# One block's 1226 tasks put in another written order (adaLN, linear attention and gated MLP on one core)

## The chip, the core and the metric

The kernel runs on one core of a Trainium2 chip. The core has TensorE (PE, matrix products, whose weight loads are shown apart as PEld), VectorE (DVE), ScalarE (ACT), GpSimd (POOL) and SyncE (SP, which here only issues DMAs). Each engine works through its own queue in order; semaphores make it wait for others. The metric is the device time of one execution in microseconds, as the median of several runs; lower is better.

## The reference

One transformer block on x of 2048 tokens by 512 (bf16), one batch, conditioned on a row c.

```python
mod = (_silu(c) @ w_mod).reshape(c.shape[0], 6, 1, -1)
sa, ca, ga, sb, cb, gb = (mod[:, 0].copy(), mod[:, 1].copy(), mod[:, 2].copy(), mod[:, 3].copy(), mod[:, 4].copy(), mod[:, 5].copy())
h = _layernorm(x, axis=-1) * (1 + ca) + sa
x = x + ga * _A_ref(h, A_wqkv, A_w_phi, A_wo)
h = _layernorm(x, axis=-1) * (1 + cb) + sb
x = x + gb * _B_ref(h, B_w_gate, B_w_up, B_w_down)
```

A is linear attention with 32 heads of 16: q, k and v by wqkv; pq and pk are q and k times a 16x16 matrix for each head; phi is softmax(p) beside softmax(-p) (32 features a head); kv sums phi_k by v over all tokens, z sums phi_k; the output of a head is (phi_q kv) / (phi_q z), then wo. B is a gated MLP of width 1376: (sigmoid(h w_gate) * (h w_up)) w_down.

## The kernel before

All work is cut into 1226 named tasks. `Graph.add` records for each task its engines (`alts`), what it reads and writes, and its buffers; `Graph.arrange` reads the long string `ORDER` (L40 to L87), gives each task its engine (the first of its alternatives, or the letter behind `@`: A for ACT, D for DVE, P for POOL), and hands out buffer slots in that order: 8 PSUM banks, 6 tiles `r2k`, 2 output tiles `ot`, and so on. `emit` then writes the instructions in that order. So ORDER alone sets each engine's queue, SP's DMA queue among them, and which earlier task must be done before a slot is used again.

The tasks, with the lines that the profile names:

- SP loads `ld_*`: `x0a` to `x3a` are tokens (256 KB for two tiles of 128, x3a 512 KB), `wk0`, `wk1` halves of the key weights, `wm00a` to `wm01b` the four 256 KB pieces of w_mod for sa and ca, `wmm2` 1.5 MB of w_mod for the rest, `wmga` the piece for ga, `wv0`, `wo`, `wu0`, `wg0`, `wd`, `wd2` weights. `wqT0` to `wqT3` (L798) are DMA transposes of the query weights from DRAM. `gwa`, `gra`, `gwb`, `grb` send ga and gb through DRAM to spread them over the partitions.
- `warm0` (six matmuls) and `warm1_0` to `warm1_11` (one each, L729) do no part of the result; PE runs them while it waits for data. `c1`, `c2`, `c3` make silu(c). `modc1.0` and `modc1.1` (L759) multiply it with w_mod for sa and ca and need wm00a with wm00b, and wm01a with wm01b; `modc2.0`, `modc2.1` (L745) need wmm2; `modca` needs wmga. Those with a c behind copy the result to SBUF.
- Key and query weights are folded with w_phi: `tpw` (L790) transposes, `wTc` (L793) copies, `fold` (L808) multiplies, `foldc` (L814) copies to `wqk_f`; side 1 is the keys, side 0 the queries.
- First layernorm over 16 token tiles, in nine groups (tiles 0; 1; 2,3; and so on): `st1` (L831, L832), `rs1` (L838 on ACT, L841 and L842 on POOL), `nmr1` (L847), `xn1` (L856, L860), transposes `tph` on PE (L873; for the groups of tiles 10 to 13 a DMA `xT1`, L865), `hm1` (L880 on ACT, L882 elsewhere) with the modulation.
- For each token tile t: `K` (L899; with a and b in two halves for t under 8), `e` (exp, ACT, L920), `n` (sums, DVE, L923), `r` (reciprocal; L936 on DVE, L933 and L934 on ACT), `phi` (product, POOL or DVE, L926), `V` (L903), `va` (copy, L949), `kv` (L287; adds into two PSUM banks over all tiles). Tiles 11, 13, 14 and 15 go in parts. Then `kvm`, `kvp`, `kvz`, `kvn` (L308 to L338) mask and reorder kv.
- `Q` and `qe` (L987, L992) for four chunks of 512 tokens by four blocks. Then for each unit of one or two tiles: `sm`, `smS`, `den` (L421 to L430) or, from tile 8 on, `z` and `dn` (L380 to L404); `num` (L457, L373), `u` (L463, L446, L448), `o` and `oT` (L481, a DMA transpose L484; on PE as `tpo` for tiles 0 and 1), `out` (L490), `x1` (L495, adds x), `st2` (L499, L500), `rs2`, `nmr2`, `xn2` (L532, L534), `xnT` (L541; on PE for tiles 0 and 1, L549), `mod` (L556 to L560). `wo` and `wd` (L967, L976) scale weights with ga and gb on POOL.
- MLP over six chunks of 1, 1, 2, 4, 4 and 4 tiles and eleven blocks of the width: `g` and `u` with a dot (L581, and L583, L586 for the last block), `tg` (tanh, ACT, L591), `hm` with a dot (DVE, L599 to L602), then `y` (eleven matmuls a tile, L619), `fin` (adds x, DVE, L626) and `st` (store, L628). The last tile, 15, goes in two parts, 384 columns and 128 columns (`b`).
- `bnd*` (L640 to L659) work out a bound on the weights and `ldf` reads the flag; above it another program part, `general`, would be run. It isn't run here.

What ORDER says goes through these two lines:

```python
t.eng = LETTER[e] if e else next(iter(t.alts))
assert t.eng in t.alts and t.deps <= done and t not in done, name
```

Of the kernel before, what the change touches and what calls it, by code (L numbers as in the profile page):

```python
# [1175 lines left out]
```

## Time and profile before

| | |
|---|---|
| median of 3 runs | 208.11 us (208.02 to 208.42) |
| span of the profiled execution | 207.1 us, mean granted TensorE clock 0.997 |
| PE, DVE, ACT, POOL busy, share of the span | 97%, 81%, 52%, 49% |
| DMA | 18.75 MB, mean 91 GB/s |
| instructions | 4382 |

In the fences below, a line of the timeline is: start in us, length in us, engine, line, operation, output and input by the program's names, shapes, count (neighbours of one kind are merged), and in brackets how long the engine sat idle just before and what ended that. A line of groups is: line, engine, operation, names, shapes and count, then busy us and mean ns of one, then idle us before them. A line of waits is: who waited, for whom, total us, times, longest. A line of stretches is: from and to, length, then busy us and count for PE, PEld, DVE, ACT and POOL, the granted clock, the share of the DMA engines and GB/s. A DMA issue line ends with the KB of one and the median us from issue to landing.

### The profile page before, as it was taken

Reading aid. Unit: us, or ns where it says so; the run is one execution under the profiler, and the core shown is the slowest. Engines: PE = TensorE matmul, PEld = TensorE weight load, DVE = VectorE, ACT = ScalarE, POOL = GpSimd, SP = SyncE. Lnnn points to the kernel's source line nnn. Section 1 sums busy time; section 2 is a strip of 40 time slices with the busy share of each in tenths; the row PEclk is TensorE's granted clock in tenths of the full one; section 3 lists DMA queues with packets and bytes.
Section 4 is the critical chain, followed back from the end, with each engine's and each line's share of the span. In section 5 each row is a group of like instructions: output and inputs, shape, how many; then the busy total and the mean of one; then the engine's idle time right before and its main releaser. Section 6 shows DMA issues by size and latency. Waiting matters only on the chain.

```text
span 207.1 us, 4382 instructions
## 1 busy us (share of the span) xinstructions
PE 200.2 (97%) x1559; PEld 112.0 (54%) x1559; DVE 167.1 (81%) x456; ACT 108.4 (52%) x266; POOL 100.7 (49%) x135
## 2 busy tenths in 40 slices
...
GB/s 169 319 354 300 266 195 75 143 257 327 54 0 3 51 6 51 54 51 29 76 103 17 89 0 25 36 68 52 38 38 0 52 79 25 51 25 3 25 63 51
DMA packets 32557, 18.75 MB, mean 91 GB/s; under 512 B 21169, under 2 KB 30738, under 8 KB 32530
## 3 DMA queue, kind: packets, MB, share of 16 engines
...
## 4 chain that ended last, share of the span: by engine, by line
PE 73%; DVE 9%; ACT 8%; DMA 3%; SPq 3%; issue 2%; POOL 0%; DVEq 0%; POOLq 0%
PE y_ps L619 18%; PE u_ps L581 17%; PE g_ps L581 17%; PE a_ps L490 7%; PE q_ps L987 5%; ACT e L920 4%; DMA x_sb<-in_A_x_dram 3%; DVE st L831 3%; DVE ks L923 3%; PE num L373 2%; PE num L457 2%; SPq L676 1%; ACT h1T L880 1%; PE g_ps L583 1%; ACT vaug L949 1%
## 5 line engine op out<-in xcount | busy, mean ns | idle before, releaser
L591 ACT ACTIVATE tg<-g_ps 128x512 bf16<-128x512 f32 (+3 forms) x66 | 28.4, 454 | 58.2 <-PE g_ps L581 40.7
L619 PE MATMUL y_ps<-wd_sb,wmod_sb 128*128 128x512 bf16 (+4 forms) x187 | 44.7, 367 | 0.0
L602 DVE SCALAR_TENSOR_TENSOR wmod_sb<-tg,u_ps 128x512 bf16<-128x512 bf16 (+4 forms) x63 | 30.1, 493 | 12.6 <-ACT tg L591 8.0
L581 PEld LDWEIGHTS <-wg_sb 128*128 128x128 bf16 (+1 forms) x252 | 21.7, 99 | 15.1
L581 PEld LDWEIGHTS <-wu_sb 128*128 128x128 bf16 (+1 forms) x252 | 21.6, 99 | 15.0 <-issue 0.4
L926 POOL TENSOR_TENSOR phi<-e,ks 128x1024 bf16<-128x1024 bf16 (+2 forms) x18 | 28.0, 1565 | 2.3 <-DVE phi L926 1.8
L619 PEld LDWEIGHTS <-wmod_sb 128*128 128x128 bf16 (+1 forms) x187 | 17.3, 98 | 16.4 <-issue 0.2
L481 POOL TENSOR_TENSOR o<-u 128x512 bf16<-128x512 f32 x12 | 15.2, 1270 | 22.4 <-DVE u L446 12.6
L581 PE MATMUL u_ps<-wT_sb,wu_sb 128*128 128x512 bf16 (+2 forms) x124 | 24.0, 322 | 0.0
L581 PE MATMUL g_ps<-wT_sb,wg_sb 128*128 128x512 bf16 (+2 forms) x124 | 23.6, 322 | 0.0
L581 PE MATMUL u_ps<-wqk_sb,wu_sb 128*128 128x256 bf16 (+4 forms) x128 | 19.9, 287 | 0.0
L923 DVE TENSOR_REDUCE ks<-e 128x64 f32<-128x1024 bf16 (+2 forms) x22 | 19.6, 896 | 0.2
L920 ACT ACTIVATE e<-k_ps 128x512 bf16<-128x512 f32 (+2 forms) x44 | 19.5, 547 | 0.3 <-PE k_ps L899 0.2
L581 PE MATMUL g_ps<-wqk_sb,wg_sb 128*128 128x128 bf16 (+4 forms) x128 | 19.1, 287 | 0.0
L626 DVE TENSOR_TENSOR ot<-y_ps,x 128x512 bf16<-128x512 f32 (+2 forms) x17 | 11.0, 654 | 8.8 <-PE y_ps L619 7.5
L992 ACT ACTIVATE eT<-q_ps 128x512 bf16<-128x512 f32 x32 | 17.2, 632 | 0.1
L899 PE MATMUL k_ps<-wqk_f,h1T 128*128 128x512 bf16 x64 | 16.8, 378 | 0.0
L903 PE MATMUL v_ps<-wv_sb,h1T 128*128 128x512 bf16 x64 | 16.3, 379 | 0.0
L490 PE MATMUL a_ps<-wo_sb,oT 128*128 128x512 bf16 x64 | 16.1, 379 | 0.0
L987 PE MATMUL q_ps<-h1T,wqk_f 128*128 128x512 bf16 x64 | 15.9, 379 | 0.1
L831 DVE BATCH_NORM_STATS2 st<-x_sb 128x6 f32<-128x512 bf16 x16 | 10.7, 668 | 3.1 <-DMA x_sb<-in_A_x_dram 3.1
L976 POOL TENSOR_TENSOR wd_sb<-wd_sb,wmod_sb 128x512 bf16<-128x512 bf16 x11 | 12.7, 1168 | 0.0
...
## 6 DMA issues: line engine op xcount, KB each, us to landing
out_dram<-ot SPq DMA_DIRECT2D x15, 128.0 KB, 1.7
...
wd_sb<-in_B_w_down_dram SPq DMA_DIRECT2D x1, 1280.0 KB, 10.4
...
```

What stands on the lines that cost most here:

```text
L490: pe.matmul(ap_[:], lhsT=oT[:, j, :], rhs=wo_sb[:, j, :], start=(j == 0), stop=(j == KT - 1))
L581: pe.matmul(ps[:fsz, 0:n], lhsT=w[:, j, ft * P:ft * P + fsz], rhs=h[:, j, 0:n], start=(j == 0), stop=(j == KT - 1))
L591: G.add(f"tg{k}.{ft}", {"ACT": 0.13 + n * 0.00083}, lambda e, tg=tg, g_ps=g_ps, fsz=fsz, n=n: act.activation(tg[:fsz, 0:n], g_ps[:fsz, 0:n ...
L602: dve.scalar_tensor_tensor(hm_all[:fsz, hm[k].slot, ft, 0:n], tg[:fsz, 0:n], 1.0, u_ps[:fsz, 0:n], op0=ALU.add, op1=ALU.mult)
L619: mm = pe.matmul(y[:, 0:c1 - c0], lhsT=hm_all[:fsz, hm[k].slot, ft, tl * P:(tl + 1) * P], rhs=wd_sb[:fsz, ft, c0:c1], start=(ft == 0), sto ...
L831: dve.bn_stats(st1[:, t, :], x_sb[:, t, :])
L899: pe.matmul(kp[:], lhsT=h1T[:, j, t * P:(t + 1) * P], rhs=wqk_f[:, j, D:2 * D], start=(j == 0), stop=(j == KT - 1))
L920: act.activation(ee[:, ha:hb, s, :], kp[:, ha * DH:hb * DH].rearrange("p (h j) -> p h j", j=DH), ACT.Exp, scale=1.0 - 2.0 * s)
L923: dve.tensor_reduce(ks[:, ha:hb].rearrange("p h s -> p (h s)"), ee[:, ha:hb].rearrange("p h s j -> p (h s) j"), axis=AX.X, op=ALU.add)
L926: engine(e).tensor_tensor(ph[:, ha * 32:hb * 32].rearrange("p (h j) -> p h j", j=DH), ee[:, ha:hb].rearrange("p h s j -> p (h s) j"), ks[: ...
L987: pe.matmul(qp[:], lhsT=wqk_f[:, j, blk * P:(blk + 1) * P], rhs=h1T[:, j, cq * 512:(cq + 1) * 512], start=(j == 0), stop=(j == KT - 1))
L992: act.activation(eT[cq][:, s * 4 + blk, :], qp[:], ACT.Exp, scale=1.0 - 2.0 * s)
```

## The change

ORDER is replaced as a whole; nothing else in the file is. The same 1226 tasks stand in another order, and 94 of them name another engine: 17 go from ACT to POOL, 14 from POOL to ACT, 26 from DVE to ACT, 26 from ACT to DVE, 7 from POOL to DVE and 4 from DVE to POOL. PE's tasks and the matmuls in them are the same. The beginning and the end of both strings:

```diff
--- before.py
+++ after.py
@@ -38,52 +38,52 @@
 ORDER = """
-wdz warm0 c1 warm1_0 warm1_1 warm1_2 warm1_3 warm1_4 ld_x0b st1_3 st1_2 c2 rs1_2 ld_x0a ld_wk1 tpw2 st1_1 rs1_1 pmem bd wTc2 tpw3 warm1_5 warm1_6 nmr1_2 st1_0
-c3 ld_wk0 wTc3 tpw0 tpw1 warm1_7 ld_x1a nmr1_1 st1_4 xn1_2 xn1_3 wTc0 rs1_0 ld_wm00a ld_wm00b xn1_1 ld_wm01a fold13 fold12 warm1_8 warm1_9 tph21 fold10 tph20
-st1_5 wTc1@D rs1_3@P ld_wm01b xn1_0 modc1.0 fold11 warm1_10 foldc13 foldc12 foldc10 modc1c0@D ld_x2a ld_x1b ld_wv0 hm1_20 hm1_21 warm1_11 tph01 tph03 tph00
-tph11 foldc11 hm1_00@A modc1.1 tph02 K3a modc1c1 hm1_01 nmr1_3 xn1_5 xn1_4 hm1_11@A st1_9 st1_8 rs1_5@P tph10 tph22 tph23 K2a K0a hm1_03@A hm1_02@A hm1_22@A
-K0b st1_7 st1_6 rs1_4@P tph30 tph33 ld_x2b hm1_23@A K3b V3a V3b K2b tph13 ld_x3a hm1_33 nmr1_5 e0.0 hm1_10@A st1_10 e3.0 tph12 V2a V2b V1a hm1_12@A va3
-hm1_13@A nmr1_4 n0.0 tph32 hm1_32 hm1_30 tph31 r0.0 xn1_9 n3.0 xn1_6 xn1_7 xn1_8 V0a V1b K1a tph42 V0b phi0.0 va2 hm1_31@A e2.0 va1 ld_wmm2 st1_11 va0 tph41
-K1b e1.0 tph40 r3.0@A K4a tph43 n2.0 K5a hm1_42 K5b tph53 hm1_53 modc2.0 rs1_6@P modc2.1 hm1_41@A hm1_43@A hm1_40@A modc2c r2.0@A n1.0 tph51 hm1_51 wqT0 wqT3
-ld_wmga tph52 kv0.0 K4b e4.0 V5 fold03 hm1_52@A nmr1_6 phi3.0 foldc03 e5.0 phi2.0 st1_15 r1.0 st1_13 st1_14 V4 va4 rs1_8 phi1.0 xn1_11 n4.0 nmr1_8 ld_wd wqT1
-ld_wd2 V6 modca.0 K6a modca.1 tph50 xn1_10@A modcac K7a K7b hm1_50 r4.0 kv1.0 kv2.0 K6b st1_12 K8 V9 e7.0 va6 e6.0 n5.0 xT1_10 xT1_11 rs1_7 va9 gwb wqT2 r5.0
-xn1_14 xn1_15 kv3.0 tph82 tph80 phi4.0 va5@D nmr1_7 hm1_80 K9 V7 e8.0 xn1_12@A xT1_12 kv4.0 V8 phi5.0 hm1_60 hm1_61 xn1_13@A xT1_13 n7.0 hm1_82 r7.0 n6.0
-kv5.0 hm1_62@P hm1_63@P K10 tph83 ld_wo e9.0 va7 V10 K11 tph81 hm1_83@A phi7.0 e10.0 va8@D r6.0 n8.0 hm1_81 phi6.0 r8.0 V11 fold02 V14 hm1_70 hm1_73 hm1_71
-foldc02 kv6.0 hm1_72@P phi8.0 K14 kv7.0 e11.0 n9.0 va14 e11.6 e11.2 e11.4 r9.0 K13 kv8.0 K12 n10.0 n11.0 r10.0 n11.6 n11.4 va10 e14.0 e14.4 wmod_free phi9.0
-n11.2 fold00 foldc00 r11.4 r11.2 r11.6 n14.0 V13 kv9.0 fold01 phi10.0 e12.0 foldc01 e13.0 va11 r11.0 va13@D r14.0 V12 gwa Q03 Q00 phi11.4 kv10.0 n12.0 phi11.2
-phi11.0 kv11.0 kv11.2 r12.0 qe03 e13.4 n14.4 r14.4@A ld_wu0 ld_wg0 grb va12 K15 kv11.4 phi11.6 e15.4 n13.0 r13.0 n13.4 V15 kv11.6 r13.4@A e15.0 qe00 Q10 Q01
...
-g5.7 tg5.7 hm5.1 g5.8 hm5.7 fin9 u5.8 g5.5 tg5.4 u5.0 y11.7 g5.10 st8 g5.0 y11.8 bnd0 bnd2 tg5.8 hm5.8 u5.5 tg5.0 hm5.0 y11.9 u5.4 hm5.4 bndb g5.3 tg5.5 tg5.3
-y11.10 fin11 hm5.5 u5.3 hm5.3 g5.6 u5.10 u5.6 tg5.6 hm5.6 y13.0 y13.1 y13.2 y13.3 y13.4 y13.5 y13.6 y13.7 tg5.10 y15.0b bndc hm5.10 st9 st11 bndd y15.1b y15.0
-y15.2b y15.1 y15.3b y15.4b y13.8 y13.9 y13.10 y15.5b y15.6b y15.7b fin13 y15.8b y15.2 y15.3 y15.4 y15.5 y15.6 y15.9b st13 y15.7 y15.8 y15.10b y15.9 y15.10
-fin15b y12.0 st15b fin15 st15 ldf y14.0 y14.1 y14.2 y14.3 y14.4 y14.5 y14.6 y14.7 y14.8 y12.1 y14.9 y14.10 fin14 st14 y12.2 y12.3 y12.4 y12.5 y12.6 y12.7
-y12.8 y12.9 y12.10 fin12 st12
+wdz warm0 c1 warm1_0 c2 warm1_1 ld_x0b pmem warm1_2 st1_3 st1_2 warm1_3 bd warm1_4 ld_x1a warm1_5 warm1_6 st1_5 st1_4 ld_wk0 tpw1 tpw0 rs1_2@P nmr1_2 rs1_3@P
+ld_x0a ld_wk1 wTc0 st1_1 wTc1 nmr1_3 xn1_3 fold10 xn1_5 tpw3 warm1_7 st1_0 rs1_0@P ld_x2a xn1_4 tpw2 foldc10 wTc3 fold13 warm1_8 c3 wTc2 fold12 ld_wm00a
+ld_wm00b st1_8 xn1_2@A rs1_1 nmr1_1 xn1_0 warm1_9 warm1_10 tph21 modc1.0 tph00 tph20 warm1_11 tph01 ld_wm01a ld_wm01b foldc12 st1_9 foldc13 xn1_1 modc1c0
+hm1_20@A fold11 tph03 tph30 foldc11 ld_x1b hm1_21 hm1_30 ld_x2b tph11 hm1_11 modc1.1 hm1_00@A tph10 tph12 tph32 tph22 modc1c1@D hm1_10 wqT0 ld_wv0 hm1_01@A
+rs1_5@P hm1_12@A hm1_03 nmr1_5 tph13 hm1_13@A xn1_9 xn1_8 K2a tph02 hm1_02@A hm1_22@A st1_6 st1_7 tph23 K3a hm1_23@A K0a tph33 K0b K1a hm1_32@A e0.0 K2b tph53
+tph52 K1b K3b rs1_4@P st1_10 st1_11 rs1_6@P hm1_53 hm1_33 nmr1_4 ld_x3a ld_wmm2 hm1_52@A e2.0 tph31 V0a e1.0 V1a V1b hm1_31 nmr1_6 tph51 n0.0 tph50 V0b fold00
+hm1_51 e3.0 foldc00 r0.0@A n1.0 hm1_50 xn1_7 V4 xn1_6 xn1_11 xn1_10 phi0.0 tph43 V2a tph40 wqT2 wqT1 n2.0 st1_14 hm1_43@A r1.0@A va4 va0 V3a V2b V3b hm1_40@A
+va2 tph41 K4a phi1.0 K5a r2.0 hm1_41 tph42 K4b n3.0 K5b hm1_42@A st1_15 e4.0 modc2.0 K6a va3 modc2.1 r3.0@A kv0.0 xT1_11 wqT3 phi2.0 xT1_10 ld_wmga ld_wu0
+rs1_8 va1 modc2c gwb phi3.0 e5.0 K9 K7a kv1.0 K7b fold02 n4.0 K8 kv2.0 V5 nmr1_8 r4.0 st1_13 phi4.0 st1_12 xn1_14 hm1_62 e7.0 n5.0 K6b V9 kv3.0 rs1_7 nmr1_7
+va5@D V8 e8.0 e9.0 xn1_13@A xn1_12 xT1_12 ld_wd2 r5.0 fold03 n7.0 kv4.0 xn1_15 va8@D foldc02 phi5.0 V7 e6.0 r7.0 foldc03@D hm1_60@P hm1_61 hm1_63 tph83 hm1_83
+V6 modca.0 modca.1 modcac va6 tph82 kv5.0 hm1_82@A n6.0 r6.0@A xT1_13 tph80 V11 K10 K11 hm1_71 n8.0 va7@D va9@D r8.0 phi7.0 tph81 hm1_81 n9.0 hm1_73 hm1_80@A
+hm1_70 hm1_72 e10.0 phi6.0 r9.0 V10 kv6.0 kv7.0 phi8.0 e11.2 e11.4 fold01 K15 foldc01 e11.6 va10 K12 e11.0 va11 kv8.0 e12.0 V13 phi9.0 n10.0 r10.0 phi10.0 K14
+n11.6 e14.4 n11.0 n11.2 r11.2 r11.0 phi11.0 kv9.0 V12 Q03 n11.4 r11.6 r11.4 n12.0 e15.4 e15.0 e14.0 va13 n15.0 r12.0 n15.4 phi11.6 phi11.2 phi11.4 phi12.0
+kv10.0 Q02 kv11.0 K13 kv11.2 V15 qe03 r15.0@A phi15.0 r15.4 n14.0 n14.4 r14.4 r14.0 Q12 kv11.4 kv11.6 e13.4 va12 n13.4 phi14.4@D phi15.4@D phi14.0@D e13.0
+qe02 r13.4@A va15 phi13.4 kv12.0 Q01 V14 va14 Q11 Q00 perm ld_wd Q10 kv13.4 kv14.4 qe01 n13.0 r13.0 phi13.0@D kv13.0 kv15.4 kv14.0 kv15.0 kvm1 Q31 gwa grb
+ld_wo wmod_free gra kvm0 wo3 wo1 kvp2 kvp1 kvn2 kvz1 qe00 qe10 qe11 kvp0 Q33 kvz0 kvz2 sm0 kvn0 qe31 sm2 smS0@D den0 Q13 kvn1@A num01 Q30 smS2 den2 num00 Q32
+num30 wd8 wo2 qe33 num31 u01 qe13 qe30 u00 u30 wd7 u31 wo0 wo_all num20 sm1 qe32 smS1 num21 num10 tpo0 Q20 num11 oT0 qe12 o3 den1 u21 u20 out0 Q21 sm4 u11
+qe20 qe21 smS4 oT3 ld_wg0 Q23 x1_0 wd10 o2 wd0 wd2 oT2 u10 tpo1 num71 num60 st2_0 den4 num70 num61 rs2_0 oT1 out3 nmr2_0 xn2_0 u70 u71 out1 xnT0 u61 mod00
+mod01 u60 tsw Q22 mod02@A mod03@A x1_1 out2 qe22 u0.8 g0.8 g0.6 tg0.8 g0.1 tg0.6 x1_3 u0.1 u0.7 u0.6 g0.4 hm0.8 x1_2 tg0.1 hm0.1 hm0.6 sm3 g0.0 g0.7 wd3 wd1
+u0.0 g0.9 o7 st2_1 oT7 qe23 g0.2 wd5 o6 tg0.0 tg0.7 hm0.0 hm0.7 rs2_1 st2_2 tg0.9 u0.9 hm0.9 nmr2_1 u0.3 g0.10 g0.3 oT6 tg0.3 tg0.2 xn2_1 out7 y0.0 u0.2 u0.4
...
+out15 tg4.6 rs2_7 hm4.4 nmr2_7 xn2_12 tg4.2 hm4.2 x1_15 st2_15 hm4.6 tg4.5 g4.7 u4.5 hm4.5 xn2_13@P g4.8 tg4.8 tg4.7 rs2_8 y11.1 g4.3 y9.0 y9.1 u4.8 u4.7
+xnT13 xnT12 st5 nmr2_8 mod73 hm4.8 xn2_14 xn2_15@P xnT14 xnT15 g4.9 u4.3 u4.10 tg4.3 hm4.3 y8.0 y8.1 g4.10 u4.9 tg4.9 hm4.7 tg4.10 hm4.10 mod71 hm4.9 st4
+y10.0 y10.1 y10.2 y9.2 y11.2 y11.3 y11.4 y10.3 y10.4 y11.5 y10.5 y10.6 y10.7 y10.8 y10.9 y10.10 fin10 st10 mod81@A y9.3 y8.2 y11.6 y11.7 y11.8 y11.9 mod82@P
+mod72 mod80 y8.3 y8.4 mod70@A mod83 g5.4 g5.9 tg5.9 tg5.4 g5.1 u5.4 u5.9 hm5.9 u5.3 hm5.4 y8.5 g5.0 g5.8 tg5.0 y8.6 y8.7 y8.8 y8.9 y8.10 u5.1 u5.0 tg5.1 hm5.1
+bnd1 g5.3 tg5.3 hm5.3 fin8 y11.10 g5.5 tg5.5 y9.4 u5.5 g5.6 u5.2 fin11 u5.8 bnd3 hm5.0 hm5.5 tg5.8 g5.2 u5.6 y15.0 g5.7 tg5.2 hm5.2 y13.0 y13.1 y13.2 y13.3
+bnd0 bndb tg5.6 st8 y9.5 y9.6 y9.7 y9.8 y9.9 y9.10 u5.7 hm5.8 st11 hm5.6 g5.10 tg5.7 u5.10 y13.4 bndc hm5.7 y13.5 y13.6 y12.0 y12.1 y13.7 y13.8 y13.9 y12.2
+tg5.10 y12.3 y12.4 y12.5 y12.6 bndd ldf hm5.10 y12.7 y12.8 fin9 st9 y14.0 y12.9 y12.10 y14.1 y15.1 y14.2 fin12 y13.10 st12 y14.3 y14.4 y14.5 y14.6 y15.2 y14.7
+y15.3 fin13 st13 y15.4 y14.8 y14.9 y15.5 y15.6 y14.10 fin14 y15.7 y15.8 y15.9 y15.10 fin15 st14 y15.0b y15.1b y15.2b st15 y15.3b y15.4b y15.5b y15.6b y15.7b
+y15.8b y15.9b y15.10b fin15b st15b
```

The loads, in SP's old order: x0b x0a wk1 wk0 x1a wm00a wm00b wm01a wm01b x2a x1b wv0 x2b x3a wmm2 wqT0 wqT3 wmga wd wqT1 wd2 xT1_10 xT1_11; in the new: x0b x1a wk0 x0a wk1 x2a wm00a wm00b wm01a wm01b x1b x2b wqT0 wv0 x3a wmm2 wqT2 wqT1 xT1_11 wqT3 xT1_10 wmga wu0. Seven Q tasks stand ahead of the first kv of tile 13 in the new order, five in the old. The last tile stored is 15b in the new order and 12 in the old.

44 lines of the change are left out of this document (17 added, 27 removed).

## Prediction

> **What bounds the kernel now.** I read the page's first two parts, then busy time by stretches, then the waits of TensorE (PE), then the timeline of the first 60 us.
>
> ```profile
> span 207.1 us, 4382 instructions
> PE 200.2 (97%) x1559; PEld 112.0 (54%) x1559; DVE 167.1 (81%) x456; ACT 108.4 (52%) x266; POOL 100.7 (49%) x135
> 5.00:10.00 5.00, 3.93 (x50) 2.52 (x48) 4.49 (x18) 4.29 (x12) 3.41 (x5) 1.00 1.12 319
> 13.10:58.00 44.90, 43.88 (x419) 24.42 (x418) 42.50 (x90) 43.03 (x112) 41.18 (x42) 1.00 0.82 206
> 58.00:203.80 145.80, 145.72 (x1042) 81.78 (x1040) 115.35 (x338) 57.46 (x136) 51.26 (x64) 1.00 0.18 40
> L619 PE MATMUL y_ps<-wd_sb,wmod_sb 128*128 128x512 bf16 x150 | 39.4, 379 | 0.0
> 203.76 0.69 DVE L626 TENSOR_TENSOR ot<-y_ps,x 128x512 bf16<-128x512 f32 x1 [1.26 <-PE y_ps L619]
> 204.48 0.33 SPq L628 DMA_DIRECT2D out_dram<-ot  x1
> out_dram<-ot SPq DMA_DIRECT2D x15, 128.0 KB, 1.7
> ```
>
> The window rows read: stretch, its length, then busy us of PE, PEld, DVE, ACT, POOL. From 58 us to the last matmul PE is busy 145.72 of 145.80 us: no order can win there, it can only lose. From 13.1 to 58 us every engine is over 90% busy, and PE loses 1 us that this view counts (a matmul's end is modelled, so it sees only part). So the time is PE's fixed work, what PE waits ahead of 58 us, and the tail: the last addition 203.76 to 204.45, a store issued at 204.48 that lands 1.7 us later (206.2), and 0.9 us to the end of the span. The profiled execution's span is 207.1 us and the median of the runs 208.11, so I make the sum against 207.1 and add 1.0 us.
>
> **The change part by part.** The set of tasks is the same and PE runs the same 1559 matmuls; 94 tasks outside PE change engine. What counts is where PE waits.
>
> *Landings.* The input loads land one after another in the order of issue.
>
> ```profile
> 6.11 0.62 PE L790 MATMUL tp_w<-ident,wqk_sb 128*128 128x128 bf16 x8 [0.63 <-DMA wqk_sb<-in_A_wqkv_dram]
> 7.22 0.45 PEld L790 LDWEIGHTS <-wqk_sb 128*128 128x128 bf16 x8 [0.56 <-DMA wqk_sb<-in_A_wqkv_dram]
> 7.95 0.69 DVE L831 BATCH_NORM_STATS2 st<-x_sb 128x6 f32<-128x512 bf16 x1 [0.27 <-DMA x_sb<-in_A_x_dram]
> 9.79 0.50 PE L759 MATMUL modc_ps<-sc_bf,wmod_sb 128*128 128x1 bf16 x14 [0.37 <-DMA wmod_sb<-in_w_mod_dram]
> 11.57 0.41 PEld L759 LDWEIGHTS <-wmod_sb 128*128 128x128 bf16 x14 [0.22 <-DMA wmod_sb<-in_w_mod_dram]
> 12.30 0.70 DVE L831 BATCH_NORM_STATS2 st<-x_sb 128x6 f32<-128x512 bf16 x1 [0.44 <-DMA x_sb<-in_A_x_dram]
> 11.99 0.59 PE L899 MATMUL k_ps<-wqk_f,h1T 128*128 128x512 bf16 x2
> 12.70 1.46 PE L899 MATMUL k_ps<-wqk_f,h1T 128*128 128x512 bf16 x6
> ```
>
> These waits date the 3rd, 4th, 5th, 7th, 9th and 10th transfer of 256 KB: 6.1, 7.2, 7.95, 9.8, 11.55 and 12.3 us. The new order issues x0b, x1a, wk0, x0a, wk1, x2a and only then the four pieces of w_mod, so modc1.0 waits for the 8th transfer (halfway between 9.8 and 11.55: 10.7) in place of the 7th, and modc1.1 for the 10th (12.3) in place of the 9th. Behind modc1.1 (16 matmuls, 0.4 us) stand seven transposes (0.4 us) and then K2a, whose last inputs (foldc11 on ACT, hm1_21 on DVE) I find ready by 12.7. So the first key matmul starts at 13.1 us, not at 11.99. By 13.1 the old kernel has issued two halves of K (four matmuls at 0.216 us, from the six at 12.70: 1.46 less one's 0.38, by five; together 0.86 us), and the new one three transposes more (0.17 us at 0.056). **Front: +0.7 us**, between +0.2 (landings half a transfer earlier) and +1.2 (half a transfer later).
>
> *Waits taken away.*
>
> ```profile
> 21.59 0.28 PE L873 MATMUL tp_h<-ident,xn 128*128 128x128 bf16 x2
> 22.03 1.49 PE L745 MATMUL modc_ps<-sc_bf,wmod_sb 128*128 128x1 bf16 x48 [0.16 <-DMA wmod_sb<-in_w_mod_dram]
> 45.88 2.12 PE L987 MATMUL q_ps<-h1T,wqk_f 128*128 128x512 bf16 x8
> 46.31 1.19 PEld L987 LDWEIGHTS <-wqk_f 128*128 128x128 bf16 x7 [0.55 <-ACT wqk_f L814]
> 52.05 1.02 PE L987 MATMUL q_ps<-h1T,wqk_f 128*128 128x512 bf16 x4
> 53.77 0.30 PE L287 MATMUL kvacc<-vaug,phi 128*128 128x68 bf16 x4 [0.69 <-DVE phi L926]
> PEld L287 <- DVE phi L926: 1.4, 2, 1.2
> ```
>
> Four waits show. modc2.0 starts 0.32 us after its turn (two transposes from 21.59 at 0.056 end their issue at 21.71), for a landing; Q03's second matmul waits 0.22 for foldc01; kv13.0 starts at 53.77 though the four Q matmuls of 52.05 end their issue at 52.91: 0.86, for phi on DVE; and kv15.0 once more about 0.27 (the second wait in the PEld row). Sum 1.67 us.
>
> In the new order modc2.0 has 44 matmuls of 512 columns and 27 transposes between it and K2a: 44 x 0.216 + 27 x 0.056 = 11.0, so PE is there at 24.1 us, two later than the landing that ends at 22 now (one 128 KB transpose more ahead of it). foldc01's place on ACT comes to 41.5 us by the sum of its rows and Q03's on PE to 45.1. Ahead of kv13.4 now stand seven Q blocks and not the five ahead of kv13.0: with 156 matmuls of 512 columns, 104 of 68 at 0.032 and the small ones PE arrives at 13.1 + 41.5 = 54.6. DVE's queue up to the masking keeps 88 tasks of the same sum (fifteen out, fifteen in, within 0.2 us by their rows), and its last phi now ends at 53.7 and 55.5; the wait is covered by Q work. If DVE were 1 us later than that, this cover is gone again and 0.86 comes back. **Taken away: -1.7 us**, from -0.8 (kv13 returns) to -2.3 (small waits of under 0.1 us go too).
>
> *Waits added.* xnT0 moves up past Q20 and Q22 on PE.
>
> ```profile
> L495 DVE TENSOR_TENSOR x<-a_ps,x_sb 128x512 f32<-128x512 f32 x16 | 10.7, 679 | 0.0
> L499 DVE BATCH_NORM_STATS2 st<-x 128x6 f32<-128x512 f32 x16 | 10.9, 683 | 0.1
> L428 DVE TENSOR_REDUCE den<-m 128x64 f32<-128x128 f32 x3 | 0.9, 289 | 0.1
> L429 DVE RECIPROCAL den<-den 128x64 f32<-128x64 f32 x3 | 1.7, 553 | 0.1
> L534 ACT ACTIVATE xn<-x,nmr,rs 128x512 bf16<-128x512 f32 x6 | 4.9, 810 | 1.8 <-DVE nmr L517 1.7
> ```
>
> From out0 to xnT0 DVE does x1_0 (0.68), u10 (0.6), st2_0 (0.87), den4 (1.4, two more like the 0.29) and nmr2_0 (0.2), and ACT xn2_0 (0.81): 4.6 us, with the handovers 4.9. PE has Q21, Q23, out3 and out1 (16 at 0.216), sm4 (16 at 0.025), tpo1 and four num (24 at 0.056) between: 5.2. I take +0.2 (0 to 0.6), since DVE comes to x1_0 behind u11; Q22 and out2 queue behind xnT0 and only move. Elsewhere past 58 us DVE has 30 us of slack, ACT 88 and POOL 94, so engine swaps cost nothing there.
>
> *The tail.*
>
> ```profile
> L626 DVE TENSOR_TENSOR ot<-y_ps,x 128x384 bf16<-128x384 f32 x1 | 0.6, 558 | 0.0
> L626 DVE TENSOR_TENSOR ot<-y_ps,x 128x128 bf16<-128x128 f32 x1 | 0.3, 292 | 0.8 <-PE y_ps L619 0.8
> out_dram<-ot SPq DMA_DIRECT2D x1, 32.0 KB, 2.0
> ```
>
> The last addition becomes the 128-column one (0.29 and not 0.69), but it follows the 384-column one (0.56), which starts only 0.6 us ahead of PE's end, two stores are issued one behind the other at 0.35 to 0.5, and the small store lands in 2.0 and not 1.7. Gains and losses of 0.3 to 0.4 cancel: **0.0**, from -0.3 to +0.6 (if fin15 waits for st13's landing, whose buffer it takes).
>
> Sum: +0.7 - 1.7 + 0.2 + 0.0 = **-0.8 us**, span 206.3, time **207.3 us**.
>
> **Rivals.**
>
> *POOL becomes the bound of the key stage (slower).*
>
> ```profile
> L842 POOL TENSOR_TENSOR rs<-ve,mhalf 128x2 f32<-128x2 f32 x4 | 2.9, 733 | 0.3
> 19.69 1.93 POOL L926 TENSOR_TENSOR phi<-e,ks 128x1024 bf16<-128x1024 bf16 x1
> 40.16 11.22 POOL L926 TENSOR_TENSOR phi<-e,ks 128x1024 bf16<-128x1024 bf16 x9
> 47.84 0.55 PE L287 MATMUL kvacc<-vaug,phi 128*128 128x68 bf16 x12
> ```
>
> Ahead of phi0 POOL gets rs1_2 and rs1_0 more (1.0 each, 0.73 by this row and 0.22 for the addition ahead of it) and xn1_2 less (0.75), and xn1_9 waits behind nmr1_5, itself behind modc1.1: by my sum phi0 starts at 21.2, not 19.69, and as less stands between the phis later, phi10 ends near 45.3 (now 40.16 + 3 x 1.92 = 45.9). But PE is at kv10.0 at 13.1 + 32.9 = 46.0, not 47.84: the margin falls from 2.0 to 0.7 us. Past 0.7 us of further lateness PE waits one for one; POOL has no slack to make it up (41.18 of 44.90). With 2.4 us more, 1.7 us is lost: span 208.0, **209.0 us**. Against it: the old queue already held as many waits at the front.
>
> *The clock falls back (slower).*
>
> ```profile
> 1.25 2.74 PE L729 MATMUL warm<-wd_sb 128*128 128x512 bf16 x6 [1.25 <-DVE wd_sb L722]
> 4.11 1.37 PE L729 MATMUL warm<-wd_sb 128*128 128x512 bf16 x5
> ```
>
> Six warm matmuls take 2.74 us at the start and five 1.37 us later: PE begins at half rate. Between the last warm matmul and K2a the new order has under 2 us of one-column matmuls and transposes. If these don't hold the clock and one such slow phase returns at 13 us, 1.4 us is lost (2.74 less 6 x 0.216): span 207.7, **208.7 us**. The granted clock is 1.00 throughout the same kind of work at 9 to 12 us now, which speaks against it.
>
> The Trainium skill ("TensorE: Matmul & The Clock Gate", Part 1) says that the clock halves after an idle window of about 3.4 us; by that rule the forecast stands, since no wait that I find here is that long. The same page of the Trainium skill (Part 4: PE-mode transpose) says that transpose mode doesn't count as busy; by that the stretch ahead of K2a looks idle and the time would be the rival's, and no row here decides.
>
> *Nothing gained.* hm1_62 on ACT, ahead of e7.0, needs xT1_10, which stands on SP behind three transposes from DRAM.
>
> ```profile
> 11.07 7.65 SPq L798 DMA_TRANSPOSE wT_sb<-in_A_wqkv_dram  x2
> 32.30 1.19 SPq L798 DMA_TRANSPOSE wT_sb<-in_A_wqkv_dram  x1
> ```
>
> Issued into a full queue these hold SP for 3.8 us each. My sums have xT1_10 landed at 28, ACT there at 28.3 and, two tasks on, e7.0 done 0.9 us ahead of V9, which takes its bank. A landing 1.7 us later than ACT makes V9 wait 0.8: span 207.1, **208.1 us**. For it: the three are issued while 1.5 MB of w_mod still lands; against it: one issued later into an empty queue held it for 1.2 us.
>
> *All later waits go, and the front costs 0.4:* -1.9, **206.2 us**. For it: PE's waits of now all stand in places that moved.
>
> **How the numbers follow.** About 0.2% (0.4 us) is what a measurement of this kernel can tell from no change, so faster means under 207.7. Chances: my sum 0.48 (0.44 faster, 0.04 same), POOL 0.17, clock 0.09 (both slower), nothing gained 0.16 (0.13 same, 0.03 slower), all waits gone 0.10. That is 0.54 faster, 0.17 same, 0.29 slower. The range 206.1 to 209.0 leaves out half of the best case and part of the two slow ones.
>
> **What would show it.** modc1.0 and modc1.1 waiting at 10.7 and 12.3 us, K2a at 13.1; no PE wait at modc2.0 and ahead of kv13; a short one at xnT0; the last addition 128 columns wide. Wrong if PE waits at a kv with POOL as releaser, if matmuls 0.43 us apart return after 5 us, if V9 waits near 31 us, or if PE waits past 75 us.

## The result, and the profile after

The new order is slower: 210.19 us (209.34 to 211.5, four runs) against 208.06 for the old order beside it, a ratio of 1.010 (95% interval 1.0054 to 1.0145). Forecast were 207.3 us, with 0.29 for slower. The profiled execution of the new order took 209.34 us, the shortest of its four runs.

The page of the kernel after, the lines that answer to those of before:

```profile
span 207.5 us, 4380 instructions
PE 200.6 (97%) x1559; PEld 112.1 (54%) x1559; DVE 166.4 (80%) x459; ACT 108.2 (52%) x262; POOL 101.5 (49%) x137
```

Busy time says nothing: PE is 97% busy in both. Busy time by stretches does; first the kernel after, then the kernel before (from and to, length, then busy us of PE, PEld, DVE, ACT, POOL, clock, DMA share, GB/s):

```profile
4.10:14.00 9.90, 8.31 (x99) 5.12 (x97) 9.11 (x32) 7.05 (x18) 7.79 (x13) 1.00 1.15 294
14.00:30.00 16.00, 16.00 (x161) 9.38 (x160) 15.72 (x38) 15.87 (x43) 14.69 (x15) 1.00 1.10 273
30.00:57.50 27.50, 27.50 (x260) 15.31 (x257) 25.15 (x49) 26.43 (x71) 25.65 (x25) 1.00 0.39 126
57.50:80.00 22.50, 21.64 (x262) 14.57 (x260) 20.72 (x57) 18.16 (x42) 18.51 (x19) 1.00 0.35 88
```

```profile
4.10:14.00 9.90, 8.64 (x102) 5.32 (x100) 8.68 (x31) 7.51 (x22) 5.98 (x8) 1.00 1.09 322
14.00:30.00 16.00, 15.84 (x172) 9.41 (x171) 15.76 (x39) 15.49 (x40) 14.92 (x16) 1.00 1.21 274
30.00:57.50 27.50, 26.64 (x240) 14.35 (x239) 25.88 (x50) 26.14 (x69) 25.31 (x26) 1.00 0.59 166
57.50:80.00 22.50, 22.50 (x292) 16.50 (x291) 21.00 (x58) 20.39 (x50) 16.93 (x17) 1.00 0.11 22
```

From 14 to 57.5 us PE now loses nothing that this view counts, as forecast. It lost 1.02 there before. But it loses 0.86 us from 57.5 to 80, where it lost none, and more ahead of 14 us. The waits of PE in the kernel after (who, for whom, total us, times, longest; the first stands at the start of both kernels) and the timeline of its queue and SP's at the one past 57 us, with the landing times of oT's fourteen transposes:

```profile
PE warm L729 <- DVE wd_sb L722: 1.2, 1, 1.2
PE fold_ps L808 <- ACT wT_sb L793: 1.2, 2, 0.7
PE a_ps L490 <- DMA oT<-o: 0.8, 1, 0.8
PE tp_h L873 <- DVE xn L858: 0.3, 1, 0.3
```

```profile
65.01 1.20 SPq L484 DMA_TRANSPOSE oT<-o  x1
66.26 0.57 SPq L693 DMA_DIRECT2D wg_sb<-in_B_w_gate_dram  x1
67.36 9.24 SPq L484 DMA_TRANSPOSE oT<-o  x3
71.36 1.02 PE L987 MATMUL q_ps<-h1T,wqk_f 128*128 128x512 bf16 x4
73.19 1.04 PE L490 MATMUL a_ps<-wo_sb,oT 128*128 128x512 bf16 x4 [0.81 <-DMA oT<-o]
DMA to landing us min/median/max: 2.4/2.4/5.8
```

The new ORDER has `oT3 ld_wg0 ... oT2` on SP. The 1376 KB of w_gate are issued at 66.26, the transpose oT2 at 67.36, and it lands behind them, 5.8 us after its issue, where the median of the fourteen is 2.4. out2 on PE waits for it. In the old order w_gate was issued at 40.3 us.

The front of PE's timeline after:

```profile
4.11 2.23 PE L729 MATMUL warm<-wd_sb 128*128 128x512 bf16 x7
6.39 0.62 PE L790 MATMUL tp_w<-ident,wqk_sb 128*128 128x128 bf16 x8
7.69 0.40 PE L808 MATMUL fold_ps<-bd,wT_sb 128*128 128x128 bf16 x4 [0.68 <-ACT wT_sb L793]
9.25 0.40 PE L808 MATMUL fold_ps<-bd,wT_sb 128*128 128x128 bf16 x4 [0.50 <-ACT wT_sb L793]
10.57 0.54 PE L759 MATMUL modc_ps<-sc_bf,wmod_sb 128*128 128x1 bf16 x16
11.45 0.34 PE L873 MATMUL tp_h<-ident,xn 128*128 128x128 bf16 x3 [0.34 <-DVE xn L858]
12.55 0.54 PE L759 MATMUL modc_ps<-sc_bf,wmod_sb 128*128 128x1 bf16 x16
13.53 0.59 PE L899 MATMUL k_ps<-wqk_f,h1T 128*128 128x512 bf16 x2
```

The first key matmul starts at 13.53 us, not at the 13.1 forecast. Ahead of modc1.0 PE stands twice for a copy on ACT: fold10 for wTc0, whose input tpw0 PE has only just made, and fold13 for wTc3, which stands on ACT behind foldc10. The old order kept other matmuls between these.

To count small waits too, I took from every matmul's start to the next what that shape usually needs (its lower quartile) and summed what was left, by stretches. A matmul at half rate so counts as 0.21 us lost. The second profiles lack 25 of the 1559 matmul records; there the sum goes across the gap. us of PE lost:

| us | old, 1st profile | old, 2nd (e5) | new, 1st profile | new, 2nd (e1) | forecast change |
|---|---|---|---|---|---|
| 4.1 to 14 | 2.10 | 1.95 | 3.20 | 3.52 | +0.7 |
| 14 to 57.5 | 2.57 | 1.80 | 0.74 | 0.74 | -1.7 |
| 57.5 to 80 | 0.29 | 0.28 | 1.55 | 1.47 | +0.2 |
| 80 to 95 | 0.0 | 0.0 | 0.03 | 1.36 | 0 |
| last matmul to end of span | 3.77 | 3.76 | 3.42 | 3.60 | 0.0 |
| span | 207.1 | 206.2 | 207.5 | 209.3 | -0.8 |

### The profile page after: what moved, and what is told of

Its sections match the earlier page's. It is cut to its first block, busy times and chain, and to the rows that moved or that the text cites. A ratio compares the mean times of both kernels' runs of the same rounds, so it can differ in the third digit from the quotient of the medians.

```text
span 207.5 us, 4380 instructions
## 1 busy us (share of the span) xinstructions
PE 200.6 (97%) x1559; PEld 112.1 (54%) x1559; DVE 166.4 (80%) x459; ACT 108.2 (52%) x262; POOL 101.5 (49%) x137
## 4 chain that ended last, share of the span: by engine, by line
PE 82%; DMA 7%; DVE 4%; POOL 2%; SPq 2%; issue 1%; ACT 1%; DVEq 0%
PE g_ps L581 17%; PE u_ps L581 17%; PE y_ps L619 14%; PE k_ps L899 7%; PE v_ps L903 7%; PE a_ps L490 6%; PE q_ps L987 4%; DMA oT<-o 3%; DMA wmod_sb<-in_w_mod_dram 2%; DMA out_dram<-ot 2%; PE kvacc L287 2%; PE num L373 2%; PE tp_h L873 1%; PE g_ps L583 1%; POOL o L481 1%; DVE u L463 1%
## 5 line engine op out<-in xcount | busy, mean ns | idle before, releaser
L591 ACT ACTIVATE tg<-g_ps 128x512 bf16<-128x512 f32 (+4 forms) x66 | 29.1, 453 | 61.5 <-PE g_ps L581 40.7
L481 POOL TENSOR_TENSOR o<-u 128x512 bf16<-128x512 f32 x13 | 16.7, 1288 | 17.4 <-DVE u L446 10.8
L581 PE MATMUL u_ps<-wT_sb,wu_sb 128*128 128x512 bf16 (+2 forms) x124 | 23.3, 322 | 0.0
L581 PE MATMUL u_ps<-wqk_sb,wu_sb 128*128 128x128 bf16 (+4 forms) x128 | 20.0, 287 | 0.0
L581 PE MATMUL g_ps<-wqk_sb,wg_sb 128*128 128x128 bf16 (+4 forms) x128 | 19.8, 287 | 0.0
L920 ACT ACTIVATE e<-k_ps 128x512 bf16<-128x512 f32 (+2 forms) x44 | 18.2, 518 | 0.2 <-PE kvacc L287 0.2
L899 PE MATMUL k_ps<-wqk_f,h1T 128*128 128x512 bf16 x64 | 16.1, 379 | 0.0
L510 POOL TENSOR_SCALAR ve<-mv 128x2 f32<-128x2 f32 (+1 forms) x8 | 1.8, 224 | 28.8 <-DVE mv L500 19.7
L495 DVE TENSOR_TENSOR x<-a_ps,x_sb 128x512 f32<-128x512 f32 x16 | 10.9, 685 | 2.5 <-PE a_ps L490 2.5
```

Of the source, the lines that this page charges most:

```text
L481: G.add(f"o{t}", {"POOL": 1.3, "DVE": 0.62}, lambda e, ub=ub, o=o: engine(e).tensor_tensor(o[:], ub[0][:].rearrange("p h d -> p (h d)"), u ...
L581: pe.matmul(ps[:fsz, 0:n], lhsT=w[:, j, ft * P:ft * P + fsz], rhs=h[:, j, 0:n], start=(j == 0), stop=(j == KT - 1))
L591: G.add(f"tg{k}.{ft}", {"ACT": 0.13 + n * 0.00083}, lambda e, tg=tg, g_ps=g_ps, fsz=fsz, n=n: act.activation(tg[:fsz, 0:n], g_ps[:fsz, 0:n ...
L899: pe.matmul(kp[:], lhsT=h1T[:, j, t * P:(t + 1) * P], rhs=wqk_f[:, j, D:2 * D], start=(j == 0), stop=(j == KT - 1))
L920: act.activation(ee[:, ha:hb, s, :], kp[:, ha * DH:hb * DH].rearrange("p (h j) -> p h j", j=DH), ACT.Exp, scale=1.0 - 2.0 * s)
```

## Experiments

**Both orders again.**

> The new order once more, unchanged. Theory A (the loss sits at fixed places: 1.0 us at out2, whose transposed input oT2 is issued behind the 1.4 MB load of w_gate, and about 1.1 us in the first 13 us): 210.2 us again, a wait of 0.8 to 1.0 us at out2 near 73 us and the first key matmul at 13.5 us in this profile too. Theory B (the front is unsteady: the profiled execution of 207.5 us span was a good one of 207.5 to 209.8): the first key matmul starts more than 0.5 us away from 13.53, or another wait of about 1 us shows that the first profile does not have. Theory C (the loss lies outside the span): time minus span is again about 1.75 us, and smaller by 0.5 or more for the old order.

> The old order, unchanged, for a second profile and the spans of its runs. In the runs of the old order so far the span was 206.3 us in the median, and the profiled execution that the prediction was made from had 207.1. Theory A (that execution was one of the slower ones, as the first profile of the new order was one of the faster): a span nearer 206.3 here, with one of its waits shorter or gone, and no wait of over 0.5 us between 80 and 95 us. Rival (its waits are the same in every run and the difference lies past the last matmul): the same waits to 0.1 us, and the last matmul at the same place.

The new order gave 210.23 us, the old one 207.9. Time less span is 1.71 to 1.78 us in the mean for every kernel of this study, so nothing of the loss lies outside the span (theory C falls). The spans show that the two first profiles lie to opposite sides of their medians: the old order's runs beside this one have 206.4 us in the median, and the profile that I predicted from had 207.1; the new order's ten runs have 208.45, and its first profile had 207.5. The second profile of the old order has no wait at modc2.0 and 0.37 us in place of 0.86 at kv13.0. The second of the new order has a wait that the first lacks; its rows on POOL and PE:

```profile
85.75 1.16 POOL L976 TENSOR_TENSOR wd_sb<-wd_sb,wmod_sb 128x512 bf16<-128x512 bf16 x1
88.61 1.10 POOL L558 TENSOR_SCALAR wqk_sb<-wqk_sb,modc 128x256 bf16<-128x256 bf16 x2 [1.69 <-PE g_ps L581]
89.67 1.16 POOL L976 TENSOR_TENSOR wd_sb<-wd_sb,wmod_sb 128x512 bf16<-128x512 bf16 x1
90.88 0.38 PE L619 MATMUL y_ps<-wd_sb,wmod_sb 128*128 128x512 bf16 x1 [1.17 <-POOL wd_sb L976]
```

y0.9 on PE waits for wd9, which stands on POOL behind mod20 and mod22; mod20 stood still for 1.69 us. The releaser named there is not it: mod20's tile, brought by the transpose xnT3, landed at 88.45 us. In the trace a landing has sixteen parts, as the core has sixteen DMA engines; in e1 fifteen of xnT3's parts came by 86.50 us and the last at 88.45. The landing events for xnT3 in the profiles with the new front, and the instruction fetch (one 16 KB packet) near it, in us:

```
profile     first part   last part   fetch begins   ahead of first   fetch takes
new, 1st       86.13        86.28        86.04           0.09            0.95
e1             86.36        88.45        85.94           0.42            1.33
e2             85.70        87.37        85.32           0.38            0.95
e6             86.77        86.92        86.70           0.07            1.02
e7             86.58        88.59        86.42           0.16            0.99
e9             85.72        85.86        85.65           0.07            1.21
e10            85.21        87.18        84.82           0.39            1.19
```

Where the fetch began 0.16 us or more ahead of the first part, the last came 1.7 to 2.1 us late; at 0.09 or less it did not. (In e8 the fetch came after the landing.) One late part of sixteen fits a DMA engine that the fetch held up, and a tenth of a microsecond would then decide whether wd9 is late; no run moves the fetch alone, so this cause is argued from the times and not shown. The Trainium skill ("Runtime: NRT & Kernel Launch", Instruction fetch mechanics) says that code is refilled in 16 KB blocks and that this is mostly hidden. The packets in the table are of that size (others in the trace have 8 KB); what seems not to be hidden here is the transfer beside them.

**The wait at out2.**

```diff
-gwa grb ld_wo wmod_free gra ... smS4 oT3 ld_wg0 Q23 x1_0 wd10 o2 wd0 wd2 oT2
+gwa grb ld_wo ld_wg0 wmod_free gra ... smS4 oT3 Q23 x1_0 wd10 o2 wd0 wd2 oT2
```

> The new order with one task moved: the load of w_gate (ld_wg0) issued right behind ld_wo, 28 us earlier, so that oT3 and oT2 find an empty queue. Theory A: the wait at out2 goes from 0.97 to under 0.2 us, oT2 lands 2.4 us after its issue, and the time falls by 0.8 to 1.0 us to 209.3. Rival (what out2 waits for is only the first of several late inputs, and the next one, oT0 or x1, is as late): the wait stays over 0.5 us and the time within 0.3 us of the new order's.

209.37 us, 0.86 under the new order run beside it (ratio to the old order 1.0046, 1.0022 to 1.0071, in place of 1.0104). oT2 landed 2.41 us after its issue and out2 no longer waits; the one later wait left is y0.9's:

```profile
PE y_ps L619 <- POOL wd_sb L976: 0.8, 1, 0.8
```

This term is shown: it is worth the size of the wait.

**The wait at y0.9, and the warm matmuls, each alone.**

```diff
-mod20@P mod22@P u1.0 st2_7 mod21@A tg1.2 hm1.2 wd9 mod23@P
+wd9 mod20@P mod22@P u1.0 st2_7 mod21@A tg1.2 hm1.2 mod23@P
```

> The new order with one POOL task moved: wd9 ahead of mod20. In two profiles of three, mod20 stood still for 1.3 to 1.7 us on POOL, because one of the sixteen DMA engines that bring its tile (xnT3) was taken by a 16 KB instruction fetch; wd9 stood behind it, and PE waited 1.0 to 1.3 us for wd9 at a y matmul near 89 us. Theory A: that wait is gone and mod20 to mod23 are still done when u2.0 comes up, so the time falls by about 1 us (the two waits' mean over the runs): 209.2 to 209.5. Rival (the late tile is needed by u2.0 just as soon): the wait moves to u2.0 and the time stays at 210.0 or more.

```diff
-warm1_3 bd warm1_4 ld_x1a warm1_5 warm1_6 st1_5 st1_4 ld_wk0 tpw1 tpw0
+warm1_3 bd ld_x1a st1_5 st1_4 ld_wk0 tpw1 tpw0 warm1_4 warm1_5 warm1_6
```

> The new order with three warm matmuls (warm1_4 to warm1_6) moved behind tpw0, so that four and not seven stand ahead of the first key weight transposes. In the profiles so far full clock was granted at 5.3, 6.4, 6.7 and 7.1 us, and with seven warm matmuls ahead tpw1 started at 6.4, 6.7, 6.9 and 7.1, though its data had landed at 6.3 or before. Theory A (warm matmuls at half rate hold the front back by 0.1 to 0.7 us, which the whole front follows): tpw1 within 0.1 us of its landing whatever the clock, the first key matmul at 13.5 to 13.6 us, and the time 0.3 to 0.5 us under the new order's: 209.8. Rival (the transposes then run at half rate themselves, or later pieces of w_mod set the front anyway): 210.2, the first key matmul where it was for the same clock.

Neither paid: 210.21 (1.0108, 1.009 to 1.0127) and 210.56 (1.0128, 1.01 to 1.0157). Both did what they should: in e7 the tile was late (the table above) and y0.9 did not wait, and in e6 tpw1 starts at its landing. But the wait at out2 has grown to 1.1 and 1.4 us by the view of waits. PE came to out2 0.15 and 0.27 us sooner than in e1, and oT2, whose time is set by SP and POOL (o3, then w_gate), landed 0.19 and 0.40 us later. In both, SP took 1.73 us to issue oT3 in place of 1.20 (a fetch of 1.4 us had begun at 65.0 in e7 and 64.9 in e6), and w_gate behind it followed that much later. So what they are worth shows only with w_gate moved.

> The new order with all three moves: ld_wg0 early, three warm matmuls late, wd9 ahead of mod20. Theory A (the three costs add): 0.85 measured for the first, 0.4 and 0.9 expected for the others: 208.1 us, level with the old order, with the front's fixed part (about 1 us) as what is left against the waits that the new order saves. Rival (the costs overlap, since a later PE finds later inputs ready): 208.8 or more.

> The new order with two moves, ld_wg0 early and wd9 ahead of mod20, and all seven warm matmuls where the new order has them. Theory A (the two later waits add, and the front is the rest): 0.85 for the first and the wait at the y matmul near 89 us, which 3 of 8 profiles had, for the second: 208.9 us, 0.9 over the old order, with no wait of PE over 0.3 us between 14 us and the end. Rival (the second costs nothing in the median): 209.3 as with ld_wg0 alone.

> The kernel before this with two warm matmuls (warm1_5 and warm1_6) moved behind tpw0, so that five stand ahead of the first useful matmul, as in the old order. With four there, PE stood still 0.9 us in the profile and full clock came only at 10.2 us; with five at half rate PE reaches tpw1 at 6.25, its data lands at 6.35. Theory A (what is lost is half-rate matmuls past 6.35): tpw1 at 6.4 to 6.5 us, full clock by 7.2 us in every run, 0.2 to 0.4 us under the kernel before this, and spans within 1 us. Rival (PE idle for 0.1 to 0.7 us ahead of tpw1 puts the full clock off by a further window in some runs): spans in two groups 1.3 us or more apart, the median not lower.

With w_gate early: wd9 first 208.97 (1.0047, 1.0027 to 1.0067), with two warm matmuls late besides 208.8 (1.0038, 1.0011 to 1.0065), with three late 208.63 (1.0053, 1.003 to 1.0077). In these three profiles PE has no wait over 0.3 us past 14 us. In e10 the tile was late too, and PE did not wait: wd9's move takes that wait away (1.36 and 0.95 us in e1 and e2, two of four profiles with the new front and wd9 behind mod20). By ratio to the old order none of the three differs from w_gate alone, so what it is worth in the median is not settled.

e10 shows what else holds the front. Its w_mod pieces landed sooner (the last parts of wm00b and wm01b at 9.64 and 11.43 us, against 10.40 and 12.19 in the first profile), and tpw1 started at 5.71, not 6.39; yet the first key matmul is no earlier:

```profile
9.66 0.69 DVE L831 BATCH_NORM_STATS2 st<-x_sb 128x6 f32<-128x512 bf16 x1
10.58 0.81 DVE L858 TENSOR_SCALAR xn<-x_sb,mv,rs 128x512 bf16<-128x512 bf16 x1
11.45 0.34 PE L873 MATMUL tp_h<-ident,xn 128*128 128x128 bf16 x3 [1.02 <-DVE xn L858]
13.54 0.38 PE L899 MATMUL k_ps<-wqk_f,h1T 128*128 128x512 bf16 x1
```

PE stands 1.02 us at tph00 for xn1_0 (the row at 10.58), and DVE has no idle time over 0.15 us between 3.7 us and that row. The new order has the statistics of tile 8 (st1_8, the row at 9.66) ahead of xn1_0, the old one behind it.

The clock shows in e8's front:

```profile
4.11 1.89 PE L729 MATMUL warm<-wd_sb 128*128 128x512 bf16 x4
6.49 1.03 PE L790 MATMUL tp_w<-ident,wqk_sb 128*128 128x128 bf16 x8 [0.49 <-DMA wqk_sb<-in_A_wqkv_dram]
7.32 1.49 PE L729 MATMUL warm<-wd_sb 128*128 128x512 bf16 x3
8.60 0.63 PE L808 MATMUL fold_ps<-bd,wT_sb 128*128 128x128 bf16 x4
```

Three warm matmuls from 7.32 take 1.49 us, at half rate (2 x 0.43 and the last one's 0.63); full rate came at 10.2. In the other profiles with the new front it came between 4.0 and 7.1. e8's spans lie at 206.7 to 206.9 in five runs and at 207.3 to 208.4 in four. That PE's wait of 0.7 us here (1.13 us from the start of the fourth warm matmul to tpw1, less its 0.43) put the clock off is possible, but one profile doesn't show it; in e6, with the same order ahead of tpw1, full rate had come before the wait.

**The front alone.** In e3 the old order stands up to K2b and the new one behind it; e4 is the reverse.

> The old order up to its task K2b (about 14 us), then all that is left in the new order. Theory A: the front's share of about 1.1 us goes, the wait at out2 stays: 209.1 us. Theory B: all that the new order loses comes from an unsteady front: 207.5 to 208.2 us, and its spans lie within 0.5 us of each other. If the front has no part in it: 210.2 us.

> The new order up to its task K2b (about 14.5 us), then all that is left in the old order, with the old order's waits at modc2.0, Q03 and kv13.0. Theory A: the old order plus the front's 1.1 us: 209.2 us. Theory B: the unsteady front brings the whole loss of 2.1 us along: 210.2 us or more, with spans over 1 us apart. If the front has no part in it: 208.1 us.

e4 took 210.41 (1.0112, 1.0079 to 1.0145): 2.3 us over the old order, from the front alone. It loses 3.86 us ahead of 14 us where the old order loses 2, and it keeps the old order's wait at kv13.0:

```profile
PE kvacc L287 <- DVE phi L926: 0.7, 1, 0.7
```

So a PE that comes later doesn't by itself cover that wait; behind the same front the new middle does not have it. e3 took 211.08 (1.0142, 1.0109 to 1.0175), against the expectation: its front loses 1.81 us only, but PE then stands at the transposes of tiles 8 and 9 and longer at out2:

```profile
PE a_ps L490 <- DMA oT<-o: 1.4, 1, 1.4
PE tp_h L873 <- POOL xn L860: 1.2, 1, 1.2
```

The new middle transposes tiles 8 and 9 (tph53) right behind K2b. Its own front has x2a, the load of these tiles, ahead of w_mod; the old front has it behind.

**The old front with the new middle.** e11 is the old order up to hm1_22, then the new one with w_gate early and wd9 first, e12 the same with six tasks moved. e13 and e14 are rearrangements of e11 by a search over my own estimate of the times. The expectation speaks of 35 and 16 moves; these are the moves that shortened the estimate, and with the neutral ones 310 of the 1226 tasks stand in another succession in e13, and 354 more in e14.

> The old order up to its task hm1_22 (about 13 us), then all that is left in the new order, with ld_wg0 early and wd9 ahead of mod20. It differs from the first of this call only in the front. Theory A (the new front costs 1.6 us and the waits that the new order takes away in the middle are worth 1.2): 207.3 us, 1.6 under the first of this call and 0.6 under the old order, which would beat both kernels. Rival (the old front leaves the new middle's inputs late, and its first waits come back as others): 208 or more, with waits of over 0.3 us between 13 and 25 us.

> The kernel before this with six tasks moved near the place where the two orders meet (hm1_30, hm1_23, tph53, hm1_11, e2.0 and Q01 by 4 to 15 places), to shorten the waits of PE for hm1 and xn1 there. Theory A: 0.2 to 0.4 us under the kernel before this, 207.0. Rival (those waits lie in the shadow of the next, at K or V for an activation on ACT): the same time within 0.2 us.

> The kernel with the old front, the new order behind it, ld_wg0 early and wd9 first, in which 35 tasks between 10 and 60 us are moved so that the inputs of the new middle (xn1_8 and xn1_9 for tph53 above all) come in time behind the old front. Theory A (the front costs 1.6 us, and the middle's gain of about 1.2 can be had without it): PE waits under 0.6 us for tph53 and 206.5 to 207.3 us, under the old order by 1 us. Rival (the new middle needs tiles 8 and 9 by 15 us, which only its own front loads in time, so front and middle cannot be had apart): a wait of about 1 us at the transposes of tiles 8 and 9 again, and 208.5 or more.

> The kernel before this with 16 further moves of the same kind up to 65 us. Theory A: 0 to 0.3 us under the kernel before this. Rival: the moves find nothing real, and the time is the same or up to 0.5 us longer.

209.9, 210.27, 213.91 and 213.28 us (ratios 1.0081, 1.0097, 1.0263 and 1.0238): all slower than e9 (1.0047), which has the new front. In e11 the wait at tile 8 stays (in e12 it is 1.4 us):

```profile
PE tp_h L873 <- POOL xn L860: 1.0, 1, 1.0
```

xn1_8 waits for rs1_5, that for st1_8 and st1_9 on DVE, and those for x2a. In e13 that wait is down to 0.2, but the search had put a DMA transpose of query weights behind the load of w_up and PE's out3 behind a late u:

```profile
PE fold_ps L808 <- DMA wT_sb<-in_A_wqkv_dram: 1.8, 1, 1.8
PE a_ps L490 <- DVE u L463: 1.6, 1, 1.6
PE tp_h L873 <- POOL xn L860: 0.2, 1, 0.2
```

So none of these fronts and middles could be joined without a new wait; whether the middle's gain can be had behind the old front by a better search stays open.

**What was booked as gain, alone in the old order.** e15 moves Q02 ahead of kv13.0 and Q32 ahead of kv15.0, e18 also puts phi13.0 on POOL; e16 is the old order up to hm5.6 and the new one's tail; e17 is e15 and e16.

```diff
-kv12.0 Q12 n15.0 r15.0 phi15.0@D r15.4@A kv13.0 Q02 kv13.4 ... perm kv15.0 kvm0 qe10 qe02 Q32 kvp0
+kv12.0 Q12 n15.0 r15.0 phi15.0@D r15.4@A Q02 kv13.0 kv13.4 ... perm Q32 kv15.0 kvm0 qe10 qe02 kvp0
```

> The old order with two tasks moved on PE: Q02 ahead of kv13.0 (it stood behind it) and Q32 ahead of kv15.0, so that PE has 1.7 us of Q work in place of its waits there, which were 0.86 and 0.27 us in the first profile of the old order and 0.37 and 0.27 in the second. Theory A (these waits are PE's own and their removal pays one for one): 207.4 to 207.7 us, 0.4 to 0.7 under the old order. Rival (DVE sets the next stage: kvp0 and sm0 wait for kvz and smS behind the same phis, so that the Q work taken from there leaves the wait behind): 208.0 to 208.3, with a new wait of 0.4 us or more between 55 and 60 us.

> The old order up to its task hm5.6 (about 195 us), and what is left in the new order, which ends with the 128-column addition and store and not with a 512-column one. Theory A (from the last y matmul to the span's end the new order takes 3.4 us, the old one 3.8): 207.7 us, 0.3 to 0.4 under the old order. Rival (the prediction's 0.0: the smaller store lands no sooner): 208.0 to 208.2.

> The old order with the edits of both kernels before this. Theory A (they add): 207.1 to 207.4 us, 0.8 to 1.0 under the old order, faster than both kernels. Rival (neither pays): 208.0 to 208.3.

> The old order with Q02 and Q32 moved as in e15_old_q, and phi13.0 on POOL, which stands idle at 51.6 to 52.4 us, instead of DVE. Theory A (DVE's queue sets the end of the key stage: kvm0 at 55.2 to 55.7 us on DVE is what the first kvp matmul waits for, 0.70 us in e15): DVE has 0.69 us less ahead of kvm0, the wait falls to 0.1 to 0.3 us, and the time to 207.7 to 207.9, 0.4 to 0.6 under e15_old_q and 0.2 under the old order. Rival (POOL is as full: phi15.4 and perm behind phi13.0 come 0.5 us later, and PE waits for them): 208.2 or more, with a wait at kv15.4 or kvp in the place of the old one.

208.31 (1.0011, 0.9995 to 1.0026), 208.27 (1.0006, 0.9988 to 1.0024), 208.42 (1.0011, 0.999 to 1.0033) and 208.37 (1.0, 0.9974 to 1.0026): none differs from the old order. e15's wait at kv13.0 is gone and stands at the first kvp matmul instead. e18's rows on PE and DVE:

```profile
53.85 1.02 PE L987 MATMUL q_ps<-h1T,wqk_f 128*128 128x512 bf16 x4
54.72 0.29 PE L287 MATMUL kvacc<-vaug,phi 128*128 128x68 bf16 x4
55.04 0.44 DVE L308 TENSOR_TENSOR kvm<-kvacc,mask 128x272 bf16<-128x272 f32 x1 [0.61 <-PE kvacc L287]
55.54 0.66 PE L323 MATMUL kvp<-kvm,bdp 128*128 128x68 bf16 x16 [0.53 <-DVE kvm L308]
```

DVE had been idle 0.61 us: what it waits for is kv15.0 itself, and PE then waits for the masking of it. Q32 used to stand in that handover; I had moved the cover, not added one. So my theory that DVE's queue sets this place fell with e18. The new order has eight Q blocks ahead of the first kvp matmul where the old one has seven: room for both.

## Why the prediction was wrong

*Front, +0.7 predicted.* The direction was right, the mechanism in part wrong and the size too small: the table has +1.1 and +1.6, e4 2.3 in time. The landings came as forecast (the last parts of wm00b and wm01b at 10.40 and 12.19 us, for 10.7 and 12.3), but PE waited for neither: the view of waits has no row of modc1, and modc1.1 came at 12.55 behind PE's own chain. I counted the matmuls in that chain and not the other engines in it: ACT's copies (0.68 and 0.50 us in the rows above) and xn1_0 on DVE (0.34 in the first profile, 1.02 in e10). e10 shows that the landings don't set this front: with wm00b and wm01b 0.76 us sooner the first key matmul came at 13.54 again. Seven warm matmuls, not five, also stand ahead of the first useful one, so that tpw1 starts when they end: 6.39 us in the first profile, 6.73 in e1 by the same row, with the first key matmul at 13.53 and 13.86. The rival on the clock had the wrong place: the two key matmuls at 13.53 take 0.59 us, at full rate; the clock doesn't fall back at 13 us, it comes up at another time in each run. The Trainium skill ("TensorE: Matmul & The Clock Gate", Part 1) says that the window it is switched by runs freely, so that the switch varies by 0.5 us either way; the spread here was wider, 4.0 to 7.1.

*Waits taken away, -1.7 predicted.* Right against the profile shown (2.57 to 0.74: -1.83). But that execution was 0.75 us over the median of its runs, and part of what it waited for was its own late landing at modc2.0 and what that put off; against the second profile the gain is 1.06. e16, whose middle is the old one too, has both waits again (0.4 us at modc2.0 and 0.7 at kv13.0 by the view of waits, span 207.0), so the gain changes from run to run and its median lies open between the two. Making the sum against the span and adding 1.0 hid this: 1.75 lies outside the span, so the median run had a span of 206.35, and the waits that I took away were not all in it.

*Waits added, +0.2 predicted.* This is the step that failed, beside the front's chain above. "Q22 and out2 queue behind xnT0 and only move" looked at PE's queue and forgot SP's. The wait forecast at xnT0 (which moved past Q22 alone, not past Q20) is hardly there: 0.07 us, and 0.21 at Q22 behind it, for a u on DVE. But oT2 stands behind 1.4 MB, and out2 waits 0.7 to 1.4 us by the view of waits. e2 shows it worth 0.86.

*Past 75 us, 0 predicted.* "Engine swaps cost nothing there" counted slack in sums. wd9 on POOL had 0.44 us to spare at y0.9 (88.87 to 89.31 in the first profile), and a late tile ahead of it in the queue used that up in e1 and e2. PE waiting past 75 us was named as what would prove the forecast wrong, and it did.

*Tail, 0.0 predicted.* Not contradicted: e16's time can't be told from the old order's (1.0006, 0.9988 to 1.0024), though its span ends 0.2 us sooner behind the last matmul.

*The rivals.* POOL was not the bound: phi0 came at 21.54 us (forecast 21.2) and no kv waits for POOL. V9 didn't wait. That all later waits go was right in the middle only. Slower came from SP's queue, from the front's chain through ACT and DVE, and in some runs from a late tile at wd9; no rival named one of them.

The sum as the runs leave it, for the medians: +0.86 (e2) for w_gate ahead of oT2, about +1.4 for the front, -1.1 for the middle (by the second profile), +0.4 for small waits at Q20 and Q22, -0.2 for the tail, makes +1.4. What is left up to 2.1 fits y0.9 (1.36 and 0.95 us in two of four profiles) and the longer wait at out2 of runs with a fetch beside oT3; no run separates these two in the median. e4 gives 2.3 for the front in place of 1.4, so how the last 0.7 us is divided stays open.
